# Channel mixing in a seven-product (Strassen–Winograd) form, with merged and pinned instruction streams

## The chip, the cores and the metric

The kernel runs on one core of one Trainium2 chip. The metric is the device time of one execution in microseconds (us). Lower is better. A ratio here is the mean time of one kernel's fast runs over the mean of the other's fast runs of the same rounds, with a 95% interval. It is therefore not quite the ratio of the medians that stand beside it. A run is called slow when it is over 1.5% above the fastest of the same kernel.

"The profile" is a recording of every instruction of one execution. "The trace" is the same recording, queried in detail. PE is TensorE's matmul stream, PEld its weight loads, DVE is VectorE, ACT is ScalarE, POOL is GpSimd, SP is SyncE, which issues the transposes by DMA and the output stores; in the views its lines are marked SPq, and "x2" is two instructions merged into one line.

## The reference

Attention with projected keys and values feeds an MLP mixer. Only the sizes and the last two lines matter for the change.

```python
# batch 8, heads 8, seq 1024, head_dim 64; d_model 512, d_tok 256, d_ch 1536
k_proj = einsum('ks,bhsd->bhkd', E, k);  v_proj = einsum('ks,bhsd->bhkd', F, v)
x = softmax(q @ k_proj^T / 8) @ v_proj            # heads side by side: [8, 1024, 512]
h = relu(x^T @ w_tok1) @ w_tok2                   # token mixing
u = x + h^T
h2 = relu(u @ w_ch1) @ w_ch2                      # channel mixing: 512 -> 1536 -> 512
out = u + h2
```

## The kernel before

Work goes by batches. The *front* of a batch is attention and token mixing; it ends in u, which two DMA transposes on SyncE turn into uT, one per half-batch of 512 tokens. Channel mixing works on uT. The front of batch b+1 is woven, unit by unit, between the blocks of the channel mixing of batch b. A scheduler may order the instructions of each engine. k, v and q are double-buffered.

```python
kv_pool = ctx.enter_context(tc.tile_pool(name="kv", bufs=2))        # k_sb, v_sb, q_sb
mix_pool = ctx.enter_context(tc.tile_pool(name="mix", bufs=2))      # qT, x_sb, u_sb, hT_sb, uT0, uT1
psC = ...bufs=3...;  psA = ...bufs=2 (2 banks each)...;  psS = ...bufs=1...      # PSUM
# ... cut ...
def ch1(i, cc):                                  # first projection: 4 matmuls of 512 columns
    g_ps = psC.tile([P, S2], F32, tag="c", name="g_ps")
    for dc in range(DMC):
        nc.tensor.matmul(g_ps, wc1_sb[:, dc, cc * P : (cc + 1) * P], uT[i][:, :, dc, :],
                         start=(dc == 0), stop=(dc == DMC - 1))
    nc.scalar.activation(out=st["gT", i][:, cc, :], in_=g_ps, func=ACT.Relu)

def ch2(i, ss, part):                            # second projection: 12 matmuls of 512 columns
    # ... cut: o2_ps allocated in part 0 ...
    for cc in range(part * 4, part * 4 + 4):
        nc.tensor.matmul(o2_ps, st["gT", i][:, cc, ss * P : (ss + 1) * P], wc2_sb[:, cc, :],
                         start=(cc == 0), stop=(cc == CC - 1))
    if part == CC // 4 - 1:
        # ... cut ...
        nc.vector.tensor_add(out=o_sb, in0=o2_ps, in1=u_sb[:, si, :])
        nc.sync.dma_start(out=out_v[b, :, si, :], in_=o_sb)
# ... cut ...
units = [lambda: (q_transpose(), kv_proj()), k_transpose]           # the front of batch b > 1
# ... cut: then scores, attend, token1, token2, spread evenly over the blocks ...
```

One half-batch takes 48 such matmuls for the first projection and 48 for the second.

The softmax here doesn't subtract the row's maximum and nothing guards it: scores larger than these inputs give would overflow.

## Time and profile before

The median of two runs was 503.67 us (501.42 to 505.92).

| what | before | where it is read |
|---|---|---|
| span of the profiled run | 502.0 us | page, first line |
| TensorE busy | 91% of the span | page, part 1 |
| one batch in the middle | 54.60 us, TensorE busy 54.12 | table of stretches |
| one matmul of 512 columns, unbroken | 216 ns (10.36 us / 48) | chain of waits |
| largest single wait of TensorE | 12.4 us, for qT, at the start | list of waits |

These are lines of the profile page of the kernel before: the busy time of each engine, its share of the span and its instructions; then TensorE's and the DMA's busy tenths in 40 slices of the span; then the shares of the chain of work that ended last.

```profile
PE 455.1 (91%) x2556; PEld 221.8 (44%) x2592; DVE 165.6 (33%) x304; ACT 167.3 (33%) x275; POOL 48.9 (10%) x72
...
PE   2689945975899999999999999999999999999996
...
DMA  8999999999599249855592249505020411123102
...
PE 73%; DMA 19%; ACT 3%; DVE 2%; POOL 1%; issue 1%; POOLq 0%
```

The first ten slices are ragged and the DMA is full there; from then on TensorE is busy nearly always. TensorE is the bound, except at the start. Note also "x2556" beside "x2592": one weight load goes with each matmul, so 36 matmul records are missing from this trace.

The next lines are two stretches of the same trace: one at the start, and one whole batch. The columns are the window, its length, the busy time of each engine with its instructions, the granted TensorE clock, the DMA share and GB/s.

```profile
core 0: us, PE busy (x) PEld busy (x) DVE busy (x) ACT busy (x) POOL busy (x), PEclk, DMA share, GB/s
70.00:82.00 12.00, 0.83 (x5) 0.27 (x6) 0.00 (x0) 0.08 (x1) 0.32 (x1) 0.63 1.19 186
183.80:238.40 54.60, 54.12 (x293) 25.53 (x296) 19.98 (x36) 20.08 (x33) 4.45 (x6) 1.00 0.67 135
```

In the second stretch TensorE is busy 54.12 of 54.60 us at the full clock, while VectorE and ScalarE have 20 us of work each. There is room on them, and that room is what the change wants to spend.

Two lines of the timeline of TensorE in the kernel before (start, us, engine, line, operation, count) show how fast short matmuls with new weights each can follow one another.

```profile
253.23 0.39 PE L221 MATMUL o_ps<-vb_132,a_sb 128*128 128x130 bf16 x4
253.46 1.03 PE L364 MATMUL o_ps<-wc_sb,gT 128*128 128x512 bf16 x4
```

Four attention matmuls of 130 columns start within 0.23 us: 57 ns each. The Trainium skill, page "TensorE: Matmul & The Clock Gate", section "Back-to-back issue gap", gives columns / 2.4 + 2.5 ns for the isolated gap, which is 57 ns at 130 columns and 216 ns at 512 (estimates from that formula). The trace agrees with both.

### The profile page before, as it was taken

How to read it: one execution, taken by the hardware profiler on the slowest of the kernel's cores; microseconds unless marked ns; L12 is line 12 of the kernel's file. 1: busy time of each engine (PE TensorE's matmuls, PEld its weight loads, DVE VectorE, ACT ScalarE, POOL GpSimd, SP SyncE). 2: the span in 40 equal slices, each digit the busy share in tenths (PEclk: the TensorE clock that was granted, in tenths of full speed). 3: DMA queues.
4: the chain of work that ended last, by engine and by line, in shares of the span. 5: the costliest groups of instructions: out<-in, count | busy, mean ns of one | idle time of the engine just before them, and what ended most of it. 6: DMA issues, size and time to landing. Idle time of an engine off the chain costs nothing.

```text
span 502.0 us, 6139 instructions
## 1 busy us (share of the span) xinstructions
PE 455.1 (91%) x2556; PEld 221.8 (44%) x2592; DVE 165.6 (33%) x304; ACT 167.3 (33%) x275; POOL 48.9 (10%) x72
## 2 busy tenths in 40 slices
PE   2689945975899999999999999999999999999996
PEld 1457412532345444544444444544444444444442
DVE  2354011533134332614242423533261424241102
ACT  1136641000453316150624135231615053423150
POOL 7533101301201002100200020000000000000000
PEclk9999995997899999999999999999999999999999
DMA  8999999999599249855592249505020411123102
GB/s 124 208 204 206 198 196 180 174 204 219 140 191 196 42 140 149 172 99 137 110 195 63 67 110 189 138 16 153 1 84 1 120 49 42 43 63 106 58 27 84
DMA packets 97211, 61.48 MB, mean 122 GB/s; under 512 B 60320, under 2 KB 88480, under 8 KB 97184
## 3 DMA queue, kind: packets, MB, share of 16 engines
q0 software_dynamic: 29728, 29.63, 36.5%
q1 hardware_dynamic: 67456, 31.46, 25.1%
q8 instruction: 20, 0.33, 0.2%
q14 instruction: 7, 0.06, 0.0%
HBM read 59.24 MB, written 16.78 MB: 151 GB/s over the span
## 4 chain that ended last, share of the span: by engine, by line
PE 73%; DMA 19%; ACT 3%; DVE 2%; POOL 1%; issue 1%; POOLq 0%
PE o_ps L364 31%; PE g_ps L353 26%; DMA qT<-q_sb 6%; PE h_ps L239 5%; PE u_ps L248 4%; DMA uT_698<-u_sb 4%; DMA q_sb<-in_q_dram 4%; DMA wc_sb<-in_moe_w_ch_dram 3%; PE o_ps L221 3%; PE kv_ps L174 2%; DMA v_sb<-in_v_dram 2%; PE s_ps L209 2%; ACT gT L357 1%; DMA out_dram<-o_sb 1%; DVE kp_sb L182 1%
## 5 line engine op out<-in xcount | busy, mean ns | idle before, releaser
L364 PE MATMUL o_ps<-wc_sb,gT 128*128 128x512 bf16 x738 | 183.3, 384 | 1.7 <-issue 0.2
L357 ACT ACTIVATE gT<-g_ps 128x512 bf16<-128x512 f32 x192 | 113.0, 600 | 213.7 <-PE g_ps L353 205.3
L353 PEld LDWEIGHTS <-wc_sb 128*128 128x128 bf16 x768 | 72.6, 98 | 91.8 <-issue 13.8
L364 PEld LDWEIGHTS <-gT 128*128 128x128 bf16 x768 | 73.5, 99 | 80.2 <-issue 4.8
L371 DVE TENSOR_TENSOR o_sb<-o_ps,u_sb 128x512 f32<-128x512 f32 x64 | 44.2, 691 | 90.1 <-PE o_ps L364 83.2
L252 DVE TENSOR_TENSOR u_sb<-u_ps,x_sb 128x512 bf16<-128x512 f32 x56 | 38.6, 690 | 87.7 <-PE u_ps L248 87.7
L214 ACT ACTIVATE a_sb<-s_ps 128x1024 bf16<-128x1024 f32 x32 | 32.1, 1033 | 41.8 <-PE s_ps L209 41.8
L229 DVE TENSOR_TENSOR x_sb<-o_ps,rdn 128x512 bf16<-128x512 f32 x64 | 44.2, 691 | 2.2
L248 PE MATMUL u_ps<-hT_sb,wt_sb 128*128 128x512 bf16 x112 | 34.1, 387 | 6.7 <-DVE u_sb L252 6.7
L228 DVE RECIPROCAL rdn<-o_ps 128x8 f32<-128x8 f32 x64 | 13.1, 204 | 64.8 <-PE o_ps L221 64.8
L221 PEld LDWEIGHTS <-a_sb 128*128 128x128 bf16 x256 | 20.8, 104 | 17.1 <-ACT a_sb L214 1.6
L78 POOL DMA_DIRECT2D k_sb<-in_k_dram x18 | 13.5, 751 | 143.6 <-PE kv_ps L177 136.3
L239 PE MATMUL h_ps<-x_sb,wt_sb 128*128 128x512 bf16 x106 | 26.1, 379 | 0.3
L182 DVE CAST kp_sb<-kv_ps 64x512 bf16<-64x512 f32 x8 | 5.5, 682 | 59.8 <-PE kv_ps L177 59.8
L209 PE MATMUL s_ps<-qT,kT 64*64 64x512 bf16 x128 | 12.8, 433 | 13.4 <-DMA qT<-q_sb 12.4
L248 PEld LDWEIGHTS <-wt_sb 128*128 128x128 bf16 x112 | 16.1, 144 | 19.3 <-issue 9.5
L86 POOL DMA_DIRECT2D q_sb<-in_q_dram x18 | 13.3, 741 | 92.8 <-DMA qT<-q_sb 85.4
L177 PE MATMUL kv_ps<-v_sb,FT_sb 128*64 128x512 bf16 (+1 forms) x88 | 17.4, 354 | 5.3 <-DMA v_sb<-in_v_dram 5.3
L174 PE MATMUL kv_ps<-k_sb,ET_sb 128*64 128x512 bf16 (+1 forms) x88 | 18.3, 355 | 2.0 <-DMA k_sb<-in_k_dram 2.0
L239 PEld LDWEIGHTS <-wt_sb 128*128 128x128 bf16 x112 | 10.9, 98 | 13.3 <-issue 0.2
L243 ACT ACTIVATE hT_sb<-h_ps 128x512 bf16<-128x512 f32 x14 | 8.4, 597 | 25.2 <-PE h_ps L239 25.2
L353 PE MATMUL g_ps<-uT_698,wc_sb 128*128 128x512 bf16 x48 | 12.9, 422 | 3.6 <-DMA uT_698<-u_sb 3.6
(67 smaller groups left out, 325.2 us busy)
## 6 DMA issues: line engine op xcount, KB each, us to landing
out_dram<-o_sb SPq DMA_DIRECT2D x64, 256.0 KB, 2.1
k_sb<-in_k_dram POOLq DMA_DIRECT2D x14, 512.0 KB, 9.7
v_sb<-in_v_dram POOLq DMA_DIRECT2D x14, 512.0 KB, 11.5
q_sb<-in_q_dram POOLq DMA_DIRECT2D x14, 512.0 KB, 10.0
wc_sb<-in_moe_w_ch_dram POOLq DMA_DIRECT2D x8, 384.0 KB, 17.4
k_sb<-in_k_dram POOLq DMA_DIRECT2D x4, 256.0 KB, 7.4
v_sb<-in_v_dram POOLq DMA_DIRECT2D x4, 256.0 KB, 8.0
q_sb<-in_q_dram POOLq DMA_DIRECT2D x4, 256.0 KB, 10.0
```

The source lines that it names most:

```text
L174: nc.tensor.matmul(kv_ps[0:KP, hs], ET_sb[:, si, :], k_sb[:, hs, si, :], start=a, stop=z)
L209: nc.tensor.matmul(s_ps[dst * KP : (dst + 1) * KP, h % 2, :], kT[rows, h, :], qT[rows, h].rearrange("p j s -> p (j s)"), start=True, stop= ...
L214: nc.scalar.activation(out=a_sb, in_=s_ps, func=ACT.Exp, scale=scale)
L221: nc.tensor.matmul(o_ps[:, j // 2, (j % 2) * 2 * D1 : (j % 2 + 1) * 2 * D1], a_sb[:, h % 2, j * P : (j + 1) * P], vb[:, h // 2, h % 2].rea ...
L229: nc.vector.tensor_tensor(out=x_sb[:, :, h * D : (h + 1) * D].rearrange("p (n c) d -> p n c d", n=2), in0=o4[:, :, :, 0:D], in1=rdn[:, :, ...
L239: nc.tensor.matmul(h_ps, wt1_sb[:, si, t * P : (t + 1) * P], x_sb[:, si, :], start=(si == 0), stop=(si == NSI - 1),)
L248: nc.tensor.matmul(u_ps, wt2_sb[:, t, si::NSI], hT_sb[:, t, :], start=(t == 0), stop=(t == TC - 1),)
L252: nc.vector.tensor_add(out=u_sb[:, si, :], in0=u_ps, in1=x_sb[:, si, :])
L353: nc.tensor.matmul(g_ps, wc1_sb[:, dc, cc * P : (cc + 1) * P], uT[i][:, :, dc, :], start=(dc == 0), stop=(dc == DMC - 1),)
L357: nc.scalar.activation(out=st["gT", i][:, cc, :], in_=g_ps, func=ACT.Relu)
L364: nc.tensor.matmul(o2_ps, st["gT", i][:, cc, ss * P : (ss + 1) * P], wc2_sb[:, cc, :], start=(cc == 0), stop=(cc == CC - 1),)
L371: nc.vector.tensor_add(out=o_sb, in0=o2_ps, in1=u_sb[:, si, :])
```

## The change

The intent is to replace eight products of blocks by seven. With A the half-batch (quarters a11 to a22) and B the weights (b11 to b22):

```text
S1 = a21 + a22   S3 = a11 - a21   T1: b12 - b11 (in place)   T3 = b22 - b12
S2 = S1  - a11   S4 = a12 - S2    T2 = b22 - T1              T4 = b21 - T2
M1 = a11 b11   M2 = a12 b21   M3 = S4 b22   M4 = a22 T4   M5 = S1 T1   M6 = S2 T2   M7 = S3 T3
c11 = M1 + M2;   y = M1 + M6;   c12 = y + M5 + M3;   c21 = y + M7 + M4;   c22 = y + M7 + M5
```

This is done for both projections. Sums of products are left to PSUM: bank "x" takes M1 then M2. Before M2 is added, ScalarE copies M1 into bank "y", onto which M6, M5 and M3 are then accumulated; that copy is the *seed*. Bank "z" takes M7, then M4. VectorE and ScalarE read intermediate states of y and add them to z. Between the projections the operands of the second (the S1 to S4 of relu(...), called G here) are made by VectorE.

In counts: 96 matmuls of 512 columns per half-batch become 168 of 256. SBUF fills up, so k, v, q, qT, x and hT lose their second buffer, and uT turns in two buffers instead of four. PSUM's eight banks go 3, 3 and 2 to first projection, second projection and front. Instead of a scheduler, three streams (first projection, second projection, front) are merged by numbers on a common clock of *slots* (21 per half-batch, 42 per batch), and `pin()` makes each engine keep that order.

The diff cut to its core (the whole one replaces most of the kernel):

```diff
+    def pin():
+        for i in nc.cur_bb.bb.instructions[seen[0] :]:          # each engine keeps program order
+            if last.get(i.engine) is not None:
+                tc.add_manual_dep(i, last[i.engine], order, reason="program order")
+            last[i.engine] = i.name
 ...
-    kv_pool = ctx.enter_context(tc.tile_pool(name="kv", bufs=2))
+    one = ctx.enter_context(tc.tile_pool(name="one", bufs=1))     # k, v, q, qT, x, hT
+    two = ctx.enter_context(tc.tile_pool(name="two", bufs=2))     # u, uT, S, G
 ...
-            nc.tensor.matmul(g_ps, wc1_sb[...], uT[i][:, :, dc, :], start=..., stop=...)   # 512 columns
+    def up_product(s, n):                                         # one of seven, 4 matmuls of 256
+        nc.tensor.matmul(ps[:, c, :], w1_of(n, dd, 2 * m + c), a_of(j, n, dd),
+                         start=(n in (1, 7) and c == 0 and dd == 0), ...)
+        # n == 2: G0 = relu(x);  n == 6: ub = y;  n == 5: ua = y, G2 = relu(z + ua);  n == 3: G1 = relu(y)
+        elif n == 4:
+            add_relu(g21, ps, up[s, "b"])
+            nc.vector.tensor_add(out=G[:, 3, cs], in0=g21, in1=G[:, 2, cs])
+            nc.vector.tensor_sub(out=G[:, 5, cs], in0=G[:, 0, cs], in1=g21)
+            nc.vector.tensor_sub(out=G[:, 4, cs], in0=G[:, 3, cs], in1=G[:, 0, cs])
+            nc.vector.tensor_sub(out=G[:, 6, cs], in0=G[:, 1, cs], in1=G[:, 4, cs])
+    def down_product(j, n, t):
+            if n == 6:                                            # the seed, just before its first use
+                nc.scalar.copy(out=down[j, "y"], in_=down[j, "x"])
+        # ... 6 matmuls of 256; n == 5: VectorE writes da and o_sb; n == 6, 2, 3: ScalarE, then GpSimd
+    UP = ((1, -4), (2, -1), (6, 0), (7, 1), (5, 2), (3, 4), (4, 5))      # slots within a set of 7
+    # front of batch b, spread over 42 slots by weights:
+        unit(0.0, lambda: (start_front(b), q_transpose(b)))
+        unit(1.9, lambda: kv_proj(b, 0, H))
+        unit(0.3, lambda: (load(b + 1, "k_sb", k, 2), load(b + 1, "v_sb", v, 2)))
+        # k_transpose 0.9; scores 0.4 each; load q; attend 0.25 each half; token1 0.87; token2 0.55
```

## The prediction

> **What bounds it now.** The table of stretches shows five equal batches of 54.6 us in the middle of the span (for example 183.8 to 238.4), each with TensorE busy 54.1 us at full granted clock; VectorE is busy 20.0 and ScalarE 20.1. So there TensorE is the bound. The chain of waits puts 31% on the second projection (o_ps) and 26% on the first (g_ps). At the end of that chain 48 matmuls of 512 columns take 10.36 us: 216 ns each. One batch of channel mixing is 192 of them, 41.4 us; the attention and token mixing woven into it is the other 13.1 us. 8 x 54.6 = 437; the remaining 65 us are the start: idle TensorE until data lands, 12.4 us waiting for qT, some 10 us waiting for the first transposed u, both behind crowded DMA (utilisation full to 128 us), and a lower clock after them (0.63 to 0.90).
>
> **What the change does.**
> - It replaces 96 matmuls of 512 columns per half-batch by 84 + 84 of 256. New weights come with each matmul; the attention matmuls of 130 columns already run one per 57 ns with new weights each, so the weight load shouldn't limit at 256 columns (estimate 109 ns). 168 x 109 ns = 18.3 us against 20.7: 36.6 us per batch against 41.4. Attention and token mixing keep their TensorE time (estimate 13.1). TensorE's floor: 49.7 us per batch, 398 in all; 39 us less than now. All of it lies on the critical path, as TensorE is the chain.
> - It adds to VectorE: 96 custom add-relus reading PSUM (0.69 us, as the 512-element float32 adds), 192 bf16 adds for the G operands and 64 for S (estimate 0.33 us at two elements per cycle; the Trainium skill, "VectorE: DVE Perf Modes", section "The perf-mode tier table", gives tensor_tensor that rate in bf16 from SBUF; no such instruction is in this trace), 128 attention normalisations of 256 instead of 64 of 512. Estimate: 166 rises to about 335 us, 40 of each 50 us.
> - ScalarE: five 0.60 us passes per set instead of four per set's worth of g, plus four per half-batch of the second projection: 167 rises to about 250 us.
> - GpSimd: 48 float32 adds. The skill's "SBUF — State Buffer", section "Who interferes with whom", says they block two-input VectorE operations; this trace has no such pair.
> - The first loads change order and k, v, q lose their double buffer: batch 1's q is transposed before batch 2's loads crowd the DMA. I expect both start-up waits to shrink; the first two half-batches will instead be VectorE-bound for some 5 us.
>
> **What is lost.** All engines run in pinned order with PSUM banks turning in three, three and two. Tight spots: the seed of the second projection, its n=5 add before n=3, and the normalisations against two banks. I put their waits at 2 to 4 us per batch, and the start at about 45 us over the floor.
>
> 398 + 45 + 17 = **460 us**; 8 in 10: 438 to 487. Faster by over 2%: 0.88; within 2%: 0.07; slower: 0.05.
>
> **What would show it.** Right: channel matmuls start 109 ns apart; about 52 us per batch; TensorE over 90% busy in the middle; VectorE 60 to 80% of the span; no 10 us waits for qT or uT. Wrong: matmuls over 120 ns apart; VectorE over 90% in the middle, or TensorE's waits of over 5 us per batch naming VectorE or ScalarE.
>
> **What would make it wrong.** Bf16 adds at one element per cycle (0.59 us or more each), which would make VectorE the bound near 52 to 56 us per batch; GpSimd blocking VectorE; the custom operation slower than 0.69 us; the pinned order turning small delays of one engine into waits of all.

## The result, and the profile after

The changed kernel took 608.69 us (607.86 and 609.52), with a correct result. The ratio is 1.2099 (1.1954 to 1.2244): 21% slower, where the prediction said 460 us.

The same parts of the profile page, after the change:

```profile
PE 448.1 (74%) x3665; PEld 340.5 (56%) x3686; DVE 334.6 (55%) x784; ACT 238.2 (39%) x428; POOL 106.1 (17%) x122
...
PE   3787767776894679946799367993779868898785
...
DMA  9999139399019900399002990029800270114102
...
PE 2%; DVE 1%; ACT 0%; issue 0%; DVEq 0%
```

No engine is busy over 74% of the span. TensorE has holes in every part of it, at regular distances, and the DMA bursts at the same rhythm. The chain of work breaks off after 3% of the span here, so it says nothing; the waits have to be read one by one.

One batch in the middle (same columns as before):

```profile
247.90:322.10 74.20, 53.62 (x432) 40.41 (x433) 39.90 (x94) 28.73 (x52) 11.44 (x13) 0.93 0.52 100
```

A batch takes 74.20 us instead of 54.60. VectorE has 39.90 us of work in it, as predicted, and is idle for half of the time.

To say how much is *lost*, I summed over the trace: for each pair of successive matmuls the distance of their starts, less columns / 2.4 + 2.5 ns for the first. What is left over is put down to what the second one waited for. The rest is TensorE's *floor*.

| (worked out from the traces) | before | after | predicted |
|---|---|---|---|
| floor (records missing: 36, 21) | 421.6 us | 394.6 us | 398 |
| lost up to 130 us | 49 us | 54 us | 45 |
| lost from 130 us on | 16 us | 142 us | 17 |

Traces of variants in which all 3686 matmuls were recorded give 399.1 us as the floor after the change. So the saving on TensorE is real and of the size predicted. It was lost again, and 105 us more, in waits, nearly all of them in the steady part. The list of waits after (the waiting instruction by engine, output tile and line; the engine and tile that released it; us in total, times, longest):

```profile
PE s_ps L248 <- DMA qT<-q_sb: 46.9, 5, 12.0
...
PE oy_ps L433 <- ACT oy_ps L428: 22.2, 15, 3.7
...
PE o_ps L261 <- DVE x_sb L268: 16.8, 27, 2.1
...
PE s_ps L248 <- DVE x_sb L268: 13.7, 17, 1.9
PE oy_ps L433 <- DVE da L463: 13.5, 14, 1.5
PE gx_ps L390 <- ACT gy_ps L416: 12.4, 9, 2.1
```

There are two kinds: five waits for the DMA that transposes q, four of them of 10.7 to 12.0 us and the last of 2.4, and some eighty short ones for ScalarE and VectorE, engines that are busy 39% and 55% of the time.

**The long wait.** The timelines of TensorE and of SyncE's queue in the changed kernel around one of the four:

```profile
340.58 0.60 PE L390 MATMUL gx_ps<-uT,wc_sb 128*128 128x256 bf16 x4
353.23 0.59 PE L248 MATMUL s_ps<-qT,kT 128*128 128x512 bf16 x1 [12.05 <-DMA qT<-q_sb]
353.61 1.49 PE L433 MATMUL oz_ps<-wT,G 128*128 128x256 bf16 x6
```

```profile
334.35 9.68 SPq L297 DMA_TRANSPOSE uT<-u_sb  x1
344.13 0.53 SPq L447 DMA_DIRECT2D out_dram<-o_sb  x1
344.76 8.68 SPq L199 DMA_TRANSPOSE qT<-q_sb  x2
```

q's transpose does not wait for q; it stands behind two u transposes and a store. The first of the two, issued at 322.14, occupied SyncE for 1.3 us. The second had to wait for VectorE's last u and for a uT buffer; TensorE's last read of that buffer ended at 334.32, and at 334.35 the transpose went. It then occupied SyncE for 9.68 us, and only after it, at 344.76, could q's go. In that time the loads of the next batch's k and v were in flight, which GpSimd issued from 332.34 to 335.35 us and which take 7.6 and 12.2 us to land (medians of the page's part on DMA issues). The scores start 8.5 us after q's issue.

Here the list of SyncE's own waits misleads. It names a matmul that ended at 341.2 us as what this transpose waited for, as if the buffer had been in use until then. But that matmul is only the last one that counted up the same semaphore before the transpose ended. In this trace every u transpose after 150 us starts 0.02 us after an increment of the semaphore it waits for, this one after the read that ended at 334.32. The 9.68 us are therefore not a wait for a buffer. Over all runs the time that a u transpose occupies SyncE (after 150 us) goes with the loads in flight beside it: 1.3 to 3.6 us with none, 4.8 to 6.7 with two, 7.6 to 9.7 with four and 7.9 to 9.2 with six. In the kernel before, none of these transposes had a load beside it. In the changed kernel k and v have one buffer, so their next loads are issued just after the projection has read them (GpSimd's load of k at 332.34 waited for it), and that is when u is transposed.

**The pace.** TensorE's timeline of the changed kernel in a stretch with no wait:

```profile
305.48 0.82 PE L433 MATMUL ox_ps<-wc_sb,G 128*128 128x256 bf16 x6
306.13 0.60 PE L390 MATMUL gy_ps<-St,wT 128*128 128x256 bf16 x4
306.57 0.82 PE L433 MATMUL ox_ps<-wc_sb,G 128*128 128x256 bf16 x6
```

Six matmuls of 256 columns start in 0.65 us and four in 0.44: 109 ns each, new weights each time, as estimated. Right after the 12 us wait above, six take 1.28 us (353.61 to the next group's start at 354.89), and the granted clock of that batch is 0.93. The skill's page "TensorE: Matmul & The Clock Gate", section "What's actually happening", has the clock halved after some 3.4 us of idleness. The trace agrees that it is halved: the granted clock is 1.00 from 341.2 to 346.4 us and 0.50 from 346.5 to 356.7, so it fell some 5 us into this wait; the 3.4 us themselves no run here shows. So a long wait costs a little more than its length.

**The short waits.** They have the form of a queue. VectorE's timeline after, ahead of one wait of TensorE for "da":

```profile
323.55 0.68 DVE L373 CUSTOM_DVE_ANT_0 g<-gz_ps,ub 128x512 bf16<-128x512 f32 x1
324.26 0.42 DVE L409 TENSOR_TENSOR G<-g,G 128x512 bf16<-128x512 bf16 x1
324.61 0.42 DVE L410 TENSOR_TENSOR G<-G,g 128x512 bf16<-128x512 bf16 x1
324.94 0.41 DVE L411 TENSOR_TENSOR G<-G 128x512 bf16<-128x512 bf16 x1
325.46 0.42 DVE L412 TENSOR_TENSOR G<-G 128x512 bf16<-128x512 bf16 x1
325.81 0.68 DVE L463 TENSOR_TENSOR da<-oy_ps,u_sb 128x512 f32<-128x512 f32 x1
```

```profile
326.54 0.81 PE L433 MATMUL oy_ps<-wc_sb,G 128*128 128x256 bf16 x6 [1.24 <-DVE da L463]
```

VectorE's in-order stream has a block of 2.3 us (the add-relu and four sums). The sums can wait (e5 below delays them), and "da", which TensorE needs now, stands behind it. ScalarE's timeline in the same batch, and the wait that follows it:

```profile
259.05 0.58 ACT L231 CAST kp_sb<-kv_ps 64x512 bf16<-64x512 f32 x1 [2.81 <-DVE kp_sb L230]
260.39 0.58 ACT L233 CAST vb<-kv_ps 64x512 bf16<-64x512 f32 x1 [0.76 <-DVE vb L232]
261.00 0.60 ACT L405 ACTIVATE G<-gy_ps 128x512 bf16<-128x512 f32 x1
261.63 0.57 ACT L416 COPY gy_ps<-gx_ps 128x512 f32<-128x512 f32 x1
```

```profile
262.25 0.38 PE L390 MATMUL gx_ps<-uT,wc_sb 128*128 128x256 bf16 x2 [2.11 <-ACT gy_ps L416]
```

The seed (L416) stands behind a copy that itself waited 2.81 us for VectorE. VectorE came to its own copy (L230) only at 258.35 us, after an add-relu and the four S sums of the next half-batch, which it had worked on since 256.27. A delay travels from one queue to the next until TensorE gets it.

### The profile page after: what moved, and what is told of

Its sections match the earlier page's. It is cut to its first block, busy times and chain, and to the rows that moved or that the text cites. A ratio compares the mean times of both kernels' runs of the same rounds, so it can differ in the third digit from the quotient of the medians.

```text
span 607.4 us, 9110 instructions
## 1 busy us (share of the span) xinstructions
PE 448.1 (74%) x3665; PEld 340.5 (56%) x3686; DVE 334.6 (55%) x784; ACT 238.2 (39%) x428; POOL 106.1 (17%) x122
## 5 line engine op out<-in xcount | busy, mean ns | idle before, releaser
L433 PEld LDWEIGHTS <-G 128*128 128x128 bf16 x1344 | 131.8, 99 | 114.9 <-issue 90.1
L248 PE MATMUL s_ps<-qT,kT 128*128 128x512 bf16 x64 | 28.0, 448 | 61.5 <-DMA qT<-q_sb 46.9
L253 ACT ACTIVATE a_sb<-s_ps 128x512 bf16<-128x512 f32 x64 | 38.0, 599 | 83.6 <-PE s_ps L248 83.3
L390 PE MATMUL gx_ps<-uT,wc_sb 128*128 128x256 bf16 x384 | 58.9, 277 | 13.5 <-ACT gy_ps L416 12.4
L390 PEld LDWEIGHTS <-wT 128*128 128x128 bf16 x576 | 57.5, 101 | 18.6 <-issue 3.0
L433 PE MATMUL oy_ps<-wc_sb,G 128*128 128x256 bf16 x384 | 52.0, 272 | 13.5 <-DVE da L463 13.5
L390 PE MATMUL gy_ps<-St,wc_sb 128*128 128x256 bf16 x384 | 60.1, 281 | 0.6 <-ACT ua L402 0.2
L433 PE MATMUL oz_ps<-wT,G 128*128 128x256 bf16 x384 | 56.5, 287 | 1.9 <-DVE G L410 1.8
L268 DVE TENSOR_TENSOR x_sb<-o_ps,rdn 128x256 bf16<-128x256 f32 x128 | 54.3, 425 | 4.4
L433 PE MATMUL ox_ps<-wc_sb,G 128*128 128x256 bf16 x384 | 52.1, 273 | 0.0
L261 PE MATMUL o_ps<-vb,a_sb 128*128 128x130 bf16 x256 | 35.2, 230 | 20.3 <-DVE x_sb L268 16.8
## 6 DMA issues: line engine op xcount, KB each, us to landing
v_sb<-in_v_dram POOLq DMA_DIRECT2D x14, 512.0 KB, 12.2
```

The costliest lines, as they stand in the source:

```text
L248: nc.tensor.matmul(s_ps, kT[:, h].rearrange("p c k -> p (c k)"), st["qT"][:, h].rearrange("p j s -> p (j s)"), start=True, stop=True,)
L253: nc.scalar.activation(out=a_sb, in_=s_ps, func=ACT.Exp, scale=scale)
L261: nc.tensor.matmul(o_ps[:, 2 * jj : 2 * jj + 2].rearrange("p c d -> p (c d)"), a_sb[:, j * P : (j + 1) * P], vb[:, h].rearrange("k c d -> ...
L268: nc.vector.tensor_tensor(out=xs[b][:, 4 * half : 4 * half + 4, h * D : (h + 1) * D], in0=o_ps[:, :, 0:D], in1=rdn[:, :, None].to_broadcas ...
L390: nc.tensor.matmul(ps[:, c, :], w1_of(n, dd, 2 * m + c), a_of(j, n, dd), start=(n in (1, 7) and c == 0 and dd == 0), stop=(c == 1 and dd = ...
L433: nc.tensor.matmul(ps[:, t, :], Gs[j][:, G_OF[n], cc, t * P : (t + 1) * P], w2_of(n, cc), start=(n in (1, 7) and t == 0 and cc == 0), stop ...
```

## The experiments

My theory when I set up the experiments: (1) the long waits come from the order of SyncE's queue, in which q's transpose stands behind one that, as I then read the list, waits for a buffer; (2) the short waits come from the order of in-order queues, that is from blocks and misplaced items, not from the amount of work. The rivals: for (1), that the DMA is simply crowded by the k and v loads; for (2), that VectorE has too much to do, or that pinning as such is the fault and a scheduler would mend it.

All runs, each against the kernel before in the same rounds. Unless marked, the result was correct.

| run | median us | ratio to before (95%) | one batch, us |
|---|---|---|---|
| the change | 608.69 | 1.210 (1.195–1.224) | 74–76 |
| e1_early_q | 563.87 | 1.122 (1.111–1.133) | 62.0 |
| e2_late_loads | 573.88 | 1.142 (1.133–1.151) | 65 |
| e3_early_seed | 595.52 | 1.187 (1.176–1.197) | 72–74 |
| e4_spread_front | 605.85 | 1.206 (1.195–1.217) | 74–76 |
| e5_split_sums | 546.17 | 1.093 (1.084–1.101) | 61.3 |
| e6_scalar_order | 561.32 | 1.122 (1.113–1.131) | 66–68 |
| e7_half_sums (wrong) | 549.40 | 1.098 (1.090–1.106) | 61.7 |
| e8_all | 496.41 | 0.993 (0.984–1.001) | 53.6 |
| e9_no_pin (wrong) | 526.54 | 1.052 (1.032–1.071) | 64–65 |
| e10_order_late_loads | 540.34 | 1.081 (1.068–1.094) | 61.5 |
| f1_shifted_front | 536.33 | 1.073 (1.065–1.082) | 62.5 |
| f2_shifted_late | 512.86 | 1.027 (1.018–1.035) | 56.5 |
| g1_all_late | 494.37 | 0.983 (0.979–0.988) | 53.6 |
| g2_pin_pe | 555.49 | 1.103 (1.097–1.109) | 66–67 |
| g3_all_late_pin_pe | 541.92 | 1.075 (1.070–1.080) | 63–65 |
| g6_early_late_pin_pe | 557.40 | 1.106 (1.099–1.112) | 65–67 |
| h1_earlier_u | 486.77 | 0.976 (0.969–0.983) | 52.5 |
| h2_no_spread | 511.53 | 1.025 (1.014–1.037) | 55.5–57 |

"One batch" is the distance between the first u transposes of successive batches.

### The queue of transposes: e1_early_q and e2_late_loads

e1 puts q's transpose ten slots earlier, ahead of the u transposes in SyncE's queue, and leaves the loads where they are:

```diff
-        unit(0.0, lambda: (start_front(b), q_transpose(b)))
+        at(begin - 10, lambda: q_transpose(b))
+        unit(0.0, lambda: start_front(b))
```

> After-kernel with one move: the DMA transpose of the next batch's q is put ten slots earlier in the pinned order, ahead of the second transpose of u on the same queue. Theory 1 (head of line: q's transpose is late because it stands behind a u transpose that waits for TensorE to release its buffer): the five 9 to 12 us waits of the scores for qT vanish, 608 us falls by 45 to 58 (48 us of waits and some cold clock after them), to 550-564. Rival (the transposes are slow because batch loads crowd the DMA): most of the wait stays or moves to the u transposes, and less than 25 us is won.

e2 leaves the order and takes the crowding away, by loading the next k and v later:

```diff
-            unit(0.3, lambda: (load(b + 1, "k_sb", k, 2), load(b + 1, "v_sb", v, 2)))
+            unit(0.3, lambda: None)
+            at(begin + (16 if b > 1 else 3), lambda: (load k and v of b + 1))
```

> After-kernel with one move: the loads of the next batch's k and v are issued sixteen slots into the front instead of directly after the projection of k and v, so that no load runs while u and q are transposed; the order on the transpose queue stays. Theory 1 (head of line): q's transpose still starts only after the u transpose was released, so at least half of each 9 to 12 us wait stays; at most 25 us is won. Rival (DMA crowding): the waits for qT fall below 3 us each and 35 us or more is won.

e1 won 45 us, e2 35. In e1's list of waits there is no line for qT left. In e2's there is one:

```profile
PE s_ps L248 <- DMA qT<-q_sb: 9.5, 5, 2.4
```

Four waits of 10.7 to 12.0 us and one of 2.4 have become five of up to 2.4 us, with the order on the queue unchanged. By the marks set for e2 this is the rival, crowding: each wait is below 3 us, and 34.8 us were won where 35 were asked. SyncE's queue of e2 shows the second u transpose, which took 9.68 us above, without loads beside it:

```profile
319.91 1.91 SPq L297 DMA_TRANSPOSE uT<-u_sb  x1
...
322.98 5.81 SPq L199 DMA_TRANSPOSE qT<-q_sb  x2
```

The changed kernel itself says the same: its fifth wait, of 2.4 us, belongs to the last batch, beside which nothing is loaded. So most of the long wait, 37 of 46.9 us, is the loads; what the place in the queue costs without them is what e2 leaves, 9.5 us.

e1 met the mark of the theory, but it cannot tell the two apart, because it takes q's transposes out of the loads too. In e1 they are issued here, and the next loads only at 312.69:

```profile
285.47 5.16 SPq L201 DMA_TRANSPOSE qT<-q_sb  x2
```

A run with q's transposes first in the queue and still among the loads was not made.

### The seed's place, and the front's spacing: e3_early_seed and e4_spread_front

e3 issues the second projection's seed 3.1 slots into its half-batch, instead of at the moment of its first use:

```diff
-                nc.scalar.copy(out=down[j, "y"], in_=down[j, "x"])      # in down_product, n == 6
+        at(t0 + 3.1, lambda j=j: down_seed(j))                        # the same copy
```

> After-kernel with one move: the copy that seeds the second projection's second bank is put at slot t0+3.1 in the order instead of directly before the matmuls that add to it. Theory (the seed stands in ScalarE's queue behind copies that themselves wait for recent matmuls, and TensorE waits for it): the 15 waits on that copy, 25 us in all, fall below 4 us and the time by 15 to 25 us, to 583-593. Rival (TensorE only gets to the next VectorE wait earlier): the waits on the seed vanish, those on VectorE grow by as much, and less than 8 us is won.

e4 gives attention more slots (and the rest of the front fewer), so that the normalisations come less densely:

```diff
-                unit(0.4, lambda h=h: scores(h + 2))                  # and scores(0), scores(1)
+                unit(0.6, lambda h=h: scores(h + 2))
-                unit(0.25, lambda h=h, half=half: attend(b, h, half))
+                unit(0.5, lambda h=h, half=half: attend(b, h, half))
```

> After-kernel with other weights in the order: scores and normalisations of one batch are spread over about 23 of 42 slots instead of 15, token mixing is packed closer. Theory (two PSUM banks turn faster than VectorE can normalise between its bursts for the G operands): the 38 us that TensorE waits on x_sb before scores and attention matmuls falls by half or more, and 608 us by 12 to 30 us, with the waits on qT as they are. Rival (VectorE's total load sets these waits, wherever they lie): the same sum of waits on VectorE shows at other lines, and less than 8 us is won.

e3 took all 22 us of seed waits ("oy_ps <- ACT oy_ps") out of the list, yet the time fell by 13. Its list has, in their place:

```profile
PE o_ps L261 <- DVE x_sb L268: 16.0, 24, 2.1
...
PE gx_ps L390 <- ACT gy_ps L416: 14.6, 12, 2.1
```

The other seed's waits grew from 12.4 to 14.6, and those for "x_sb" stayed where they were. A wait that is removed is partly handed to the next queue. e4 won 3 us, which is not clear of the noise (the intervals of the two ratios overlap). The waits of scores for x_sb halved (13.7 to 6.4 us), but the squeezed token mixing now waited in its stead: 4.8 us for u_sb, 3.5 for the new uT. Alone, spacing does nothing.

### Block or amount: e5_split_sums and e7_half_sums

Both stand on e1. e5 keeps every sum and only spreads the four that followed each other, one per 0.8 to 0.9 slot:

```diff
+        for n, dt in enumerate((0.7, 1.5, 2.4, 3.3)):
+            at(base + 5 + dt, lambda s=s, n=n: g_sum(s, n))      # instead of four in a row at base + 5
```

> The kernel with q's early transpose (564 us) and one more move: the four bf16 sums for the G operands, issued in one burst of 1.7 us behind the last product of a set, are spread over the next three slots. Theory (bursts: a normalisation or an add that TensorE waits for stands behind a burst of 2.4 us on VectorE): the 38 us of waits on x_sb and the 16 us on da fall by half, the time by 15 to 35 us, to 529-549. Rival (latency: two banks are too few for a chain of matmul, reciprocal, product and release, bursts or not): both waits stay within a quarter, less than 8 us is won.

e7 leaves out two of the four sums (96 in all, 41 us of VectorE) and uses other operands in their place. Its result is wrong (relative error 0.637):

```diff
-    G_OF = {1: 0, 2: 1, 4: 2, 5: 3, 6: 4, 7: 5, 3: 6}
+    G_OF = {1: 0, 2: 1, 4: 2, 5: 3, 6: 3, 7: 5, 3: 1}
-            nc.vector.tensor_sub(out=G[:, 4, cs], in0=G[:, 3, cs], in1=G[:, 0, cs])
-            nc.vector.tensor_sub(out=G[:, 6, cs], in0=G[:, 1, cs], in1=G[:, 4, cs])
```

> Wrong result on purpose: the kernel with q's early transpose (564 us) without two of the four bf16 sums for G per set (96 instructions, 41 us of VectorE); products 6 and 3 of the second projection read other sums. If VectorE's load is what TensorE waits for: waits on x_sb and da fall by a third or more and the time by 15 to 35 us. If not: less than 8 us is won. Compared with the spread sums, which keep all the work, it tells load from bursts.

Spreading won 18 us over e1, dropping half of the work 14. Two lines of e5's waits, which were 14.1 and 13.4 us in e1:

```profile
PE s_ps L250 <- DVE x_sb L270: 6.5, 18, 1.4
...
PE oy_ps L444 <- DVE da L474: 2.9, 8, 0.9
```

In e7 the same two are 8.6 and 5.7. e5 kept all of VectorE's work and won no less than e7, which took 41 us of it away. So these waits come from the block and not from the load, and the prediction's worry of a VectorE bound does not apply. e7 by itself would not show it: it shortens the block as well, and its 14 us lie between the two marks set for it. Nor is the block everything. The third line of VectorE's, attention's own matmuls behind x_sb (16.9 us in e1), stayed at 16.7 in e5 and 16.6 in e7, and e5's waits on x_sb together fell by a quarter where half was expected.

### Removing waits that only uncover others: e6_scalar_order and e10_order_late_loads

e6 is e1 with three moves for ScalarE: the early seed of e3, its copies of k and v put ahead of VectorE's, and the second projection's products set 1.35 slots apart with a gap before the product that needs "da":

```diff
-            at(t0 + 1.5 * i, lambda j=j, n=n, t=t: down_product(j, n, t))
+            at(t0 + 1.35 * i + 1.8 * (i >= 10), lambda j=j, n=n, t=t: down_product(j, n, t))
+        at(t0 + 3.1, lambda j=j: down_seed(j))
```

> The kernel with q's early transpose (564 us) and three moves in ScalarE's favour: the early seed of the second projection, ScalarE's copies of the projected k and v and of k's transpose ahead of VectorE's, and a gap of three slots between the n=5 add and n=3 in the second projection. Theory (each wait comes of one instruction standing in a queue behind one that itself waits): the waits on the second seed (27 us), on the first seed (14) and on da (16) fall to under 10 in sum, the time by 25 to 45 us, to 519-539. Rival (the waits are handed on to the next tight spot): less than 15 us is won, and the waits on x_sb grow.

It won only 3 us over e1 (not clear of the noise), although the waits for the seed were gone, those for "da" down to 0.9 us, and those of the first projection's seed to 4.5. New in its list of waits:

```profile
PE s_ps L250 <- DVE x_sb L270: 45.8, 19, 8.8
...
DVE o_sb L469 <- DMA out_dram<-o_sb: 21.1, 4, 5.9
```

Four waits of 8 to 9 us. SyncE's and VectorE's timelines of e6 around one of them show where they come from:

```profile
311.21 9.08 SPq L299 DMA_TRANSPOSE uT<-u_sb  x1
320.39 1.57 SPq L452 DMA_DIRECT2D out_dram<-o_sb  x2
```

```profile
334.27 0.69 DVE L469 TENSOR_TENSOR o_sb<-oz_ps,da 128x512 f32<-128x512 f32 x1 [5.93 <-DMA out_dram<-o_sb]
```

A u transpose that occupies SyncE for 9.08 us, with six loads in flight, holds back the output stores behind it. The first of these, issued at 320.39, landed at 334.08 us, VectorE's next sum needed its buffer and stood 5.93 us, and the normalisations stood behind that sum. It is SyncE's queue among the loads again, by another way to TensorE. e10 tests this: e6 with e2's late loads, which let the transposes and stores land faster.

> The kernel with the moves in ScalarE's favour (561 us) and, added, the late loads of k and v. In that kernel four waits of 8 to 9 us stood where a store of the output, itself late behind a u transpose on the same queue and slow among the loads, held back a VectorE add and so TensorE. If that reading is right, the four waits vanish and the time falls by 25 to 45 us, to 516-536. If they are VectorE's own lateness, less than 10 us is won.

e10 took 540.34 us, 21 less than e6, and the four long waits are gone (the longest wait of scores for x_sb is 3.1 us in my sums). The four waits went as expected; the gain is short of the 25 to 45 us expected. The second u transposes still have q's loads beside them and occupy SyncE for 5.4 to 5.6 us.

### All moves together: e8_all, g1_all_late, h2_no_spread

e8 is e6 with the split sums of e5 and the spacing of e4. g1 adds the late loads of e2. h2 is g1 without e4's spacing.

> All moves together: q's early transpose, early seed, ScalarE's copies first, the gap before n=3, the spread sums, the spread normalisations. Theory (the waits are separate, and each is a matter of order): TensorE's waits in the steady part fall from 12 to under 5 us per batch, the batch from 62 to 53-56 us, the time to 490-520, about that of before. Rival (one shared limit): above 535.

> All moves together (496 us) and the late loads, without the shift of the front that made things worse. If late u transposes and stores among the loads are the rest of the DMA's part: the 7 us of waits for u vanish and the time falls to 482-491. Rival (the phase changed by another load slot makes new waits): 493 or more.

> The best version (494 us) without the spread of scores and normalisations, which alone won only 3 us. If a wait is only worth what is left when the others are gone: 10 us or more is lost, to 504-530, and the waits on x_sb grow. If the moves are independent: about 497.

e8 took 496.41 us: 112 us less than the changed kernel, and 67 less than e1, where e5's and e6's moves alone had won 18 and 3 over e1, and e4's 3 over the changed kernel. g1 took 494.37. h2 lost 17 us against g1, so the spacing that was worth at most 3 us alone is worth 17 among the others (attention's waits on x_sb are 9.0 us in g1 and 17.7 in h2). The moves do not add: while one queue is late for any reason, mending another is not seen. An experiment that mends one thing alone therefore does not bound from above what it is worth among others.

### Is pinning the fault? e9_no_pin, g2_pin_pe, g3_all_late_pin_pe, g6_early_late_pin_pe

e9 takes every pin away; g2 pins TensorE alone and leaves the other engines to the scheduler; g3 is g1 and g6 is e1 with late loads, both with TensorE alone pinned.

```diff
         for i in done[seen[0] :]:
+            if i.engine != nc.tensor.engine:      # g2, g3, g6;   e9: pin() returns at once
+                continue
```

> The changed kernel with the pinning of the order switched off and nothing else: the scheduler may reorder each engine's instructions. Rival theory (the seven-product form itself, with its extra VectorE and ScalarE work, is what costs, in any order): within 3% of 608 us. Theory (the hand-made order costs): a clearly different time, either way; faster than 590 would say that the pinned order was worse than an automatic one.

> The changed kernel with only TensorE's order pinned; VectorE, ScalarE, GpSimd and the transpose queue are left to the scheduler; the result stays right, as the matmul order keeps PSUM's accumulation. If the pinned order of the other queues costs: waits on x_sb, da and the two seeds (92 us) fall by half or more and the time falls under 570. If the matmul order and the banks cost: 590-610.

> All moves together with late loads, only TensorE pinned. If the scheduler orders the other queues better even than the mended hand-made order: under 482, over 4% faster than before. If no better: within 2% of the same kernel with all engines pinned.

> The changed kernel with q's early transpose and late loads, and only TensorE pinned. Against 564 us with all pinned (early transpose alone): if the pinned order of the other queues makes the short waits, 500-530; if the matmul order and banks do, 545-565.

e9 gave a wrong result (relative error 0.088), so its 526.54 us is the time of a program that does something else. I believe that without pins the matmuls of one accumulation were reordered around the one with the start flag, which is argued and not shown.

g2 is correct and faster than the change (1.103 times the kernel before, against 1.210); its waits for the first projection's seed are 3.1 us in all and those for "da" 1.8. In their place VectorE shows, once per batch, the following (VectorE's timeline of g2):

```profile
328.58 0.42 DVE L311 TENSOR_TENSOR St<-uT 128x512 bf16<-128x512 bf16 x1 [11.36 <-DMA uT<-u_sb]
```

The scheduler put the S sums of the next half-batch ahead of work that TensorE needed, and there VectorE stood 11.36 us for a uT that had not landed. It had four loads beside it and took 15.5 us from issue to landing, against 4.2 to 5.8 without loads. TensorE waited behind it, 45.6 us in six waits for the add-relu's "G". So the fault is not pinning as such, nor is it cured by this scheduler: either order has an item at the head of a queue that waits for a DMA. g3, the mended order with the scheduler on the other engines, took 541.92 us, 48 more than g1 pinned, which neither of its expectations had. g6 gained nothing over g2. But these two do not test the late loads. With GpSimd unpinned the scheduler issued the loads of k and v early again, beside the second u transpose (in g3 from 298.5 us, the transpose at 300.5; in g1 some 14 us after it), and TensorE's largest wait is again the one for "G" behind it, 37.9 us in g3 and 44.9 in g6. For the same reason g6's time, which lies in the range set for "the matmul order and the banks", does not show those to be the cause. The mended hand order beats all of them.

### How narrow the mended order is: f1_shifted_front, f2_shifted_late, h1_earlier_u

f1 is e8 with the whole front two slots earlier and a little more room for token2 (q's transpose then 8 slots ahead of it); f2 is f1 with late loads.

```diff
-        front(b, 42 * b - 46 + OFF, 42 * b - 4 + OFF)
+        front(b, 42 * b - 48 + OFF, 42 * b - 6 + OFF)
-            unit(0.55, lambda si=si: token2(b, si))
+            unit(0.7, lambda si=si: token2(b, si))
```

> All moves together (496 us) and, added, attention two slots earlier against the projections, with token mixing a little less packed. Theory: the waits for the transposed u (7 us) and for token mixing's adds (5 us) go, 496 falls by 5 to 14 us. Rival: the new phase makes other waits, within 4 us of 496.

> As the one before and, added, the late loads of k and v: transposes of u fall from 9 us and more to under 5 us each; another 0 to 6 us is won, to 480-492, 2 to 5% under the kernel before.

f1 was meant to be better and was 40 us worse than e8: 28.9 us of waits of scores for x_sb and 12.8 for kT in my sums. Late loads won 23 of that back. Two slots and a few weights decide over 8% of the time; the work is the same. Why precisely this shift meets so badly I have not followed further.

h1 leaves the front where g1 has it and only lets the first u transposes of the batch come earlier, by the weights of token mixing. g1's list had seven waits of TensorE for uT, 5.4 us in all.

```diff
-                unit(0.87, lambda t=t, part=part: token1(b, t, part))
+                unit(0.7, lambda t=t, part=part: token1(b, t, part))
-            unit(0.55, lambda si=si: token2(b, si))
+            unit(0.55 if si < NJ else 0.72, lambda si=si: token2(b, si))
```

> The best version (494 us) with token mixing's weights changed so that the first four blocks of u end some 1.2 slots earlier, attention where it was. Theory: the 6 us of waits for the transposed u vanish, 487-491. Rival (a new phase, new waits): 494 or more.

h1 took 486.77 us, the best of all and 2.5% below the kernel before (0.9755; the interval, 0.9686 to 0.9825, lies below 1 and just crosses the mark of 2%). The waits for uT went from 5.4 us in seven to 1.2 in one. One batch of h1, and its largest waits:

```profile
211.00:263.50 52.50, 50.64 (x432) 39.67 (x433) 38.94 (x94) 28.64 (x52) 11.35 (x12) 1.00 0.72 141
```

```profile
PE o_ps L263 <- DVE x_sb L270: 8.7, 20, 1.8
PE s_ps L250 <- DVE x_sb L270: 7.1, 11, 1.4
...
PE gx_ps L392 <- ACT gy_ps L427: 4.7, 15, 1.0
```

The work of each engine in a batch is that of the changed kernel (VectorE 38.94 us against 39.90, ScalarE 28.64 against 28.73). Only the order is another, and 21.7 us per batch are gone. Against the kernel before, the profiled spans differ by 17.7 us (502.0 and 484.3). By the starts of the u transposes, 10.3 us of that comes from the five steady batches from the second to the seventh (262.5 against 272.8 us), 17.7 from the batch before them (48.7 against 66.4), which in the kernel before still suffers from the start; the lead-in costs 3.1 us more, and the end, from the last batch's first u transpose on, 7.2 more.

## Why the prediction was wrong

- **TensorE's floor: right.** Predicted 398 us, measured 394.6 with 21 records missing and 399.1 with none. The 109 ns per matmul of 256 columns is what the trace shows.
- **The work of the other engines: right in sum, off in its parts.** VectorE has 334.6 us against 335 predicted, ScalarE 238 against 250. The custom add-relu took 0.69 us, as estimated. The bf16 sums took 0.42 us each, not 0.33; over 256 sums that is some 24 us more, which other estimates of mine made up for. The line of the profile after is:

```profile
L409 DVE TENSOR_TENSOR G<-g,G 128x512 bf16<-128x512 bf16 x48 | 20.4, 425 | 1.6
```

  The skill, page "VectorE: DVE Perf Modes", gives the two elements per cycle in "The perf-mode tier table", and in its section on the fixed extra latency per instruction a formula (N + 151) / 0.96 ns for float32 adds. With half of 512 for N the latter gives 424 ns (an estimate from that page); the trace has 425. I had used the first and let the fixed term shrink.
- **GpSimd blocking VectorE: did not matter.** The page "SBUF — State Buffer", section "Who interferes with whom", says that a GpSimd instruction that reads SBUF and a VectorE instruction with two SBUF inputs exclude each other. The trace fits: none of the 256 sums lies inside one of the 48 float32 adds of 1.15 us, and they overlap for 0.8 us in all, where chance would give about 10 (my count and estimate from the trace). But the sums are not stretched either, and TensorE's waits do not name it.
- **The start: nearly right in size, not in kind.** Predicted 45 us over the floor, measured 54 up to 130 us. The waits for the first qT and uT shrank as expected (qT's 12.4 us is gone), but waits for ScalarE and VectorE took their place: by the same measure the kernel before loses 49 us there, so the start as a whole did not shrink.
- **The failed step, as the prediction put it: "I put their waits at 2 to 4 us per batch".** This is the term of 17 us in 398 + 45 + 17. It measured 142 us, in the middle batch above 25.6 us instead of 2 to 4, and it is most of the error: 142 less 17 is 125 of the 149 us by which the prediction missed. The rest is the start's 9 and some 15 us that neither sum holds (before the first matmul, after the last, and pieces of under 60 ns). About 48 us of it is the wait for qT and about 94 the short waits.
- **Why it failed, first part.** I had looked at q's transpose where the kernel before had its one long wait, at the start ("batch 1's q is transposed before batch 2's loads crowd the DMA"), and called that mended. For the later batches I did not ask when the loads come. With one buffer for k and v they are issued just when u and q are transposed, and four loads in flight stretch the second u transpose from 1.8 or 1.9 us of SyncE's time to 7.9 to 9.7, with q's transpose behind it. The sign for it was in the diff: k and v lost their second buffer, and the loads were put directly after the projection that frees it. e2 and the last batch of the changed kernel show this cause; e1 removes the wait too, but not the cause alone. The place behind the u transposes, which wait for one of only two uT buffers, has the smaller part (9.5 us left in e2).
- **Why it failed, second part.** I named the tight spots rightly (the seed, the add before n = 3, the normalisations against two banks), and all three are in the list of waits. But I judged them by the utilisation of the engines, 40 of 50 us. What counts is what stands ahead in the queue at the moment of need. e5 shows this for VectorE's block of sums, e3 and e8 for ScalarE's seed, and h1 for the whole: the same work per batch in 52.50 us instead of 74.20.
- **The warning that held:** "the pinned order turning small delays of one engine into waits of all" stood last in the list of what could go wrong, with 5% for a slower kernel. g1 and h1, which are pinned too, show that it should be read with care: it is this order that does so, not pinning.
- **What stays open.** h1 still loses 3.9 us per batch, and 73 us in all, of which 46 fall before 130 us. A third uT buffer would free the second u transpose before the loads begin. It did not fit into SBUF (no run of it: at the build, the last pool wants 12 KB per partition and 11.19 are left), so the wait for a free uT could only be moved, not removed. What q's transpose would lose in front of the queue but among the loads is not measured, and why loads stretch the time that a transpose occupies SyncE is not shown. Why f1 is so much worse is not settled either.

## What to carry to other kernels

When a change trades work of the bound engine for work of others and gives up buffers for it, do not judge the others by their share of busy time: follow each in-order queue, the DMA issuing one too, and ask what stands at its head waiting for a buffer or a landing while something needed at once stands behind it, and which loads are in flight beside a transpose. When a list of waits names a releaser, check it against the start of the waiting instruction. Spread short work that nobody needs yet instead of issuing it in a block, and issue what the bound engine needs (a seed, a transposed operand) as soon as its input is there. Mend such delays together before judging any of them: here a move that won at most 3 us alone won 17 among the others, and the same work took 609 us in one order and 487 in another.

## What the Trainium skill lacked or had wrong

- Page "TensorE: Matmul & The Clock Gate", section "Back-to-back issue gap": it gives about 81 ns at 128 columns and 131 ns at 512 as the sustained pace of load-and-matmul pairs, and calls its formula the isolated gap only. Here sustained streams with new weights each time kept to the formula: 57 ns at 130 columns (in groups of four), 109 at 256, 216 at 512 (48 matmuls in 10.36 us).
- Page "VectorE: DVE Perf Modes": the formula with the fixed term of 151 cycles is given for float32 adds only, and for bf16 the page has only a breakdown at 2048 elements, with a fixed part of about the same size. It has no measured figure for short bf16 sums. These kept to the formula at two elements per cycle (425 ns at 512 elements), a gain of a factor of 1.6 over the 0.69 us of float32, not the 2 of the tier table.
- Page "DMA: Bandwidth & Descriptors": none of the pages that I read says that loads in flight stretch the time that a DMA transpose occupies the issuing engine, and so hold back all transposes and stores behind it. Here it was 1.3 to 3.6 us without loads and 7.6 to 9.7 with four (9.68 us at 334.35, and q's transposes only at 344.76). Nor is there a figure for the landing: TensorE got q's 8.5 us after its issue among loads, where the profile's median landing of these transposes is 4.9 us.
- Page "PSUM — Partial Sum Buffer", section "Summary: rules for kernel authors", says that a seed written by ScalarE or VectorE must be 0. The changed kernel seeds two banks with non-zero copies of M1 by ScalarE, after zero matmuls had written each of the six banks of the two projections once, and its results are correct in every run that kept TensorE pinned and did not leave sums out. The section "The four PSUM rules" of the same page explains when this works; the summary is stricter than that.
